# New issue intervals and urgencies for a list schedule, and float32 operands that are no longer used unsplit

## The chip, the cores and the metric

The kernel runs on one core of a Trainium2 chip. The metric is the time of the launch on the device in microseconds (us); the median of several executions is given. Four compute engines matter: TensorE (PE in the profile, with its weight loads apart as PEld) multiplies matrices, VectorE (DVE) and ScalarE (ACT) work element by element, and SyncE (SP) starts most transfers between the chip's memory and the core's buffers. GpSimd (POOL) starts some of the output transfers.

## The reference

The program is a packed attention, whose result is the input of a feed-forward network. Cut to what matters:

```python
q, k, v: (8, 8, 576, 64)      # batches, heads, positions, head size
p:       (8, 8, 32, 64)       # 32 packed queries for each head

def sm_attn(qq, kk, vv):
    s = scale * qq @ kk.T
    a = exp(s - max(s)); a = a / (sum(a) + 1e-09)
    return a @ vv

p_packed = sm_attn(p, k, v)                    # 32 rows for each head
x = sm_attn(q, p_packed, p_packed)             # 576 rows for each head
x = x.transpose(0, 2, 1, 3).reshape(4608, 512) # one row for each token
h = x @ w_in                                   # 512 -> 2048
g = where(h > 0, h, exp(min(h, 0)) - 1)        # ELU
out = g @ w_out                                # 2048 -> 512
```

## The kernel before

**Stages.** For each of 8 batches the kernel does the first attention (scores of the packed queries, maximum, exponentials, transposes on TensorE, products with v), and the second attention's scores and softmax over 32 columns, whose parts are folded with 32x32 transposes on VectorE (`s2` L695, `fold` L703, `smax` L710 to `smul` L732, `unfold` L745). The second attention's last product is not done on its own: the packed rows are multiplied with `w_in` first (`mstep`, L757, giving `m`), so that an h product of the network takes `m` and the softmax weights `a`. Then come h products, ELU and out products. Chunks of the 2048 hidden columns are 128 wide and called f, so there are 16; a batch's 576 tokens are split in two windows of 256 and 320, called halves.

**Products.** TensorE multiplies float32 in a fast rounded form, fp32r. To keep the precision, an operand x is split into a high part `hi` (x rounded) and a low part `lo` (x − hi), and a product becomes three matmuls, hi·hi, hi·lo and lo·hi: `a_hi`, `a_lo` and `m_hi`, `m_lo` in an h product (L1285), `wo` and `g` parts in an out product (L1409, L1410, L1412). An unsplit product takes plain float32 operands instead (L1278 for h, L1395 for out); in the trace each of its matmuls leaves two records. The `hi` part is a cast (L284, mostly on ScalarE), the `lo` part a subtraction on VectorE (`g` L1324, `m` L809, `a` L751).

**ELU.** For each f of a window ScalarE computes relu(−h) (L1292) and its exponential (L1298), and VectorE combines them (L1301); this last step is "the ELU" below. There are two tiles for h, so that the h product two places on writes where the ELU reads.

**Weights.** `w_in` and `w_out` arrive as 64-bit floating-point words, and are converted on the chip in blocks of 128 rows (i0 to i15, o0 to o15): a load on SP (L307), an exponent on VectorE (L312), a sign and a power on ScalarE (L324, L319), then mantissa steps on VectorE (L327, L333), a product of exponent and sign (L340) and the word (L350); for `w_out`, also the parts `hi` (L284) and `lo` (L363).

**Batches 0 and 1, and the rest.** While the weights arrive, batches 0 and 1 are worked on in turns, by the list `VISITS` of (batch, half, f from, f to). Batches 2 to 7 follow whole. From batch 2's second half on, two chunks at a time go through Strassen's scheme (L1048 for h, L1187 for out, operands of g at L1121 and L1130): 21 matmuls of 256 columns instead of 12 of 512 for an out product of the pair. Pairs named in `S_PLAIN` and `S_PLAINS` are plain, with the 12. The operands made from `w_out` for Strassen (L916 to L949) are stored to the chip's memory and loaded again for each use.

**What sets the order.** Every instruction, or short run of them, is recorded by `op(prio, on, fn, deps, take, use, after, mode)`: `on` says on which engines it may run and at what cost, `deps` what it waits for, `take` the tile that it fills. `schedule()` then walks a model of time: of the instructions that may begin, it takes the one of lowest `prio` (the urgency, counted in products of the network), puts it on its engine, and sets when the engine is next idle (`idle_at`, the cost and `GAP`) and when the result may be used (`end`, the cost and `LAG`). The order that results is the static order of each engine's queue; at run time semaphores make instructions wait. Urgencies come from numbers at the top (`T_ATT`, `LI`, `LO`, `TM`, `LOOK` and the like), and `FIRST` sets the order of the first loads.

`F_PLAIN` is the number of `w_out` chunks whose products of batches 0 and 1 are unsplit; `H_PLAIN` names the batches whose first four chunks have unsplit h products. `STAY` and `SWITCH` concern TensorE's changes between two kinds of matmuls.

Of the kernel before, what the change touches and what calls it, by code (L numbers as in the profile page):

```python
# [20 lines left out]
def packed_attention_elu_ffn(  # L21
# [55 lines left out]
    ]  # L77

    T_ATT, T_ATT1 = [11.5, 13.5, 14.0, 15.0, 16.0, 16.0], [-12, -11, -11, -10, -10, -9]
    LI, LO, LM, LOOK = 4.5, 3.0, 2.5, 3.5
    TM = [24.5, 22.0, 25.0, 26.0]

    FIRST = "i0 i1 i2 i3 k v o0 o1 q".split()
    T_S2, STAY, SWITCH = 0, 4, 0.12

    F_PLAIN, H_PLAIN = 4, [0, 1]  # L90
    T_WS, T_AS = 20, 6

    S_PLAIN = [0, 7]
    S_PLAINS = {x: [0] for x in [(3, 1), (4, 0), (4, 1), (5, 0), (5, 1), (6, 0), (6, 1), (7, 0)]}
    T_SW7 = 16
    T_ATTS = [[5, 9, 13.5, 6.5, 13.0, 23.5], [-4, -2, -2, 3, 14.5, 22.0]]
    TMS = [[22, 19.5, 27.0, 27.0], [19, 29, 30.0, 30.5]]

    T_TH, LOOK_T = 1, 1
    S_FIRST, T_SW, T_SL, T_SE, LOOK_S = (2, 1), 17, 10, 5, 6.0

# [43 lines left out]
    class Buf:  # L147
        def __init__(self, ring, make, n=1):
            self.ring, self.make, self.n, self.users, self.t = ring, make, n, [], None

        def released(self, now):
            return all(u.end is not None and u.end <= now for u in self.users)
# [4 lines left out]
    ops = []  # L157
    GAP = {"PE": 0.0, "DVE": -0.03, "ACT": 0.02, "DMA": 0.0, "POOL": 0.0, "CTL": 0.0}
    LAG = {"PE": 0.15, "DVE": 0.1, "ACT": 0.12, "DMA": 2.2, "POOL": 5.0, "CTL": 0.0}
# [12 lines left out]
    def schedule():  # L172

        todo = sorted(ops, key=lambda o: (o.prio, o.n))
        idle_at = {e: 0.0 for e in GAP}
        now, out, mode = 0.0, [], None

        def engine_for(o):

            if any(d.end is None for d in o.after) or any(  # L180
                d.end is None or d.end > now for d in o.deps
            ):
# [5 lines left out]
            spare = 2.0 if any(c.end is None for c in conv_ops) else 0.0  # L188
            e = min(o.on, key=lambda e: max(idle_at[e], now) + o.on[e] + spare * (e == "DVE"))
            return e if idle_at[e] <= now else None  # L190

        while todo:
            for n, o in enumerate(todo[:400]):
                e = engine_for(o)
# [17 lines left out]
                todo.remove(o)  # L212
                break
# [648 lines left out]
    for b in range(B):  # L862
        if b == 0:
            ts = [-40 + n for n in range(5)] + [T_S2]
        elif b < NB0:
            ts = [first_use["b", b] + t for t in T_ATT1]
        else:
            ts = [first_use["b", b] - NS + t for t in (T_ATT if b <= S_FIRST[0] else T_ATTS[b % 2])]
# [9 lines left out]
    for b in range(B):  # L878
        for c in range(NFC):
# [3 lines left out]
            else:  # L883
                t = TM if b <= S_FIRST[0] else TMS[b % 2]
# [18 lines left out]

    def s_need(u):

        return next((i for i, (b, win, _) in enumerate(order) if strassen(b, win) and u not in plain_in(b, win)), None)
# [116 lines left out]
    def strassen_pair(i, b, win, f):  # L1023
# [487 lines left out]
```

## Time and profile before

| | |
|---|---|
| median of 3 runs | 712.98 us |
| lowest, highest | 710.84, 713.93 us |
| span of the profiled execution | 710.4 us, 2.6 below the median |
| TensorE busy | 687.2 us, 97% |
| VectorE busy | 587.7 us, 83% |
| ScalarE busy | 448.1 us, 63% |
| moved by DMA | 140.19 MB, 197 GB/s |

The profile is one execution. Busy time is the time in which an engine had an instruction under way, and an engine's matmuls or vector instructions overlap a little, so that the sum of single durations can be more than the busy time. A "start to start" time is read from two rows of the timeline. In a row, "out<-in" gives the tiles, then the sizes; "x4" is the number of instructions; in brackets or behind the last bar stand the idle time ahead of them and what ended it.

### The profile page before, as it was taken

The numbers are of one execution on the slowest core, as the hardware profiler recorded it, in microseconds if no ns is written. First come the engines' busy times: TensorE is split into PE (matmuls) and PEld (weight loads), VectorE is DVE, ScalarE is ACT, GpSimd is POOL, SyncE is SP. The second block draws the span as 40 slices with busy tenths as digits, with TensorE's granted clock in tenths as the row PEclk, the third lists the DMA queues.
The fourth block names the chain that finished last, engine by engine and source line by source line (L and its number), as shares of the span: only waits on it lengthen the run. The fifth ranks groups of instructions, "written<-read, shape, count | busy, mean of one in ns | idle before, by whom it ended". The sixth has DMA issues, their size and how long they took to land.

```text
span 710.4 us, 15186 instructions
## 1 busy us (share of the span) xinstructions
PE 687.2 (97%) x5688; PEld 573.6 (81%) x5688; DVE 587.7 (83%) x1430; ACT 448.1 (63%) x963; POOL 19.4 (3%) x27
## 2 busy tenths in 40 slices
PE   2799999999999999999999999999999999999997
PEld 1444588887777888899889998889888999899986
DVE  6999998888998889776898799866798889977563
ACT  5777788887666666665466555756556655655532
POOL 0000002111021000000000000000000000000000
PEclk9999999999999999999999999999999999999999
DMA  9846555645748845646867897566867887754600
GB/s 354 291 152 216 165 177 117 140 86 124 215 94 208 285 137 179 179 145 195 297 195 260 280 306 230 185 185 203 266 220 243 278 257 226 210 189 138 204 31 30
DMA packets 72553, 140.19 MB, mean 197 GB/s; under 512 B 7200, under 2 KB 16672, under 8 KB 72224
## 3 DMA queue, kind: packets, MB, share of 16 engines
q1 hardware_dynamic: 69456, 133.72, 58.2%
q0 software_dynamic: 3024, 5.51, 5.5%
q8 instruction: 45, 0.74, 0.4%
q14 instruction: 28, 0.23, 0.1%
HBM read 116.92 MB, written 22.28 MB: 196 GB/s over the span
## 4 chain that ended last, share of the span: by engine, by line
PE 93%; DMA 3%; DVE 2%; ACT 1%; issue 0%; SPq 0%; ACTq 0%
PE psum L1187 29%; PE psum L1048 19%; PE psum L1285 8%; PE psum L1409 6%; PE psum L1410 5%; PE psum L1412 5%; PE psum L1007 5%; PE psum L796 4%; PE psum L1395 4%; PE psum L1278 2%; DMA kvq<-in_qT 2%; PE psum L650 2%; PE psum L624 1%; PE psum L695 1%; DMA k<-in_kT 1%; PE psum L554 1%
## 5 line engine op out<-in xcount | busy, mean ns | idle before, releaser
L1187 PE MATMUL psum<-sw,g 128*128 128x256 f32 x816 | 126.0, 282 | 0.0
L1187 PEld LDWEIGHTS psum<-sw,g 128*128 128x128 f32 x816 | 109.9, 188 | 6.5 <-issue 4.7
L1048 PE MATMUL psum<-a_hi,m_hi 128*128 128x320 f32 (+1 forms) x320 | 97.3, 304 | 0.0
L1048 PE MATMUL psum<-a_lo,m_hi 128*128 128x320 f32 (+1 forms) x320 | 95.4, 298 | 0.0
L1048 PE MATMUL psum<-a_hi,m_lo 128*128 128x320 f32 (+1 forms) x320 | 95.3, 298 | 0.0
L1130 DVE TENSOR_TENSOR g<-w,g 128x896 fp32r<-128x896 f32 (+1 forms) x80 | 82.0, 1026 | 13.6 <-ACT g L284 13.1
L284 ACT CAST g<-w 128x896 fp32r<-128x896 f32 (+1 forms) x80 | 71.2, 890 | 23.9 <-DVE w L1121 15.0
L1187 PE MATMUL psum<-wo_a,g 128*128 128x256 f32 (+1 forms) x390 | 72.8, 318 | 0.0
L1121 DVE TENSOR_TENSOR w<-w 128x128 f32<-128x128 f32 (+1 forms) x204 | 68.1, 334 | 5.0
L1060 ACT ACTIVATE e<-psum 128x320 f32<-128x320 f32 x96 | 42.0, 437 | 44.9 <-PE psum L1048 40.1
L1048 PEld LDWEIGHTS psum<-a_hi,m_hi 128*128 128x128 f32 x320 | 60.4, 189 | 11.3 <-ACT e L1063 5.0
L1292 ACT ACTIVATE e<-psum 128x256 f32<-128x256 f32 (+1 forms) x96 | 38.6, 404 | 43.8 <-PE psum L1285 30.2
L1187 PEld LDWEIGHTS psum<-wo_a,g 128*128 128x128 f32 x390 | 58.7, 189 | 8.0 <-issue 2.6
L1048 PEld LDWEIGHTS psum<-a_lo,m_hi 128*128 128x128 f32 x320 | 60.4, 189 | 1.6
L1048 PEld LDWEIGHTS psum<-a_hi,m_lo 128*128 128x128 f32 x320 | 60.4, 189 | 0.0
L1187 PE MATMUL psum<-wo_b,g 128*128 128x256 f32 (+1 forms) x366 | 59.6, 290 | 0.0
L1187 PEld LDWEIGHTS psum<-wo_b,g 128*128 128x128 f32 x366 | 50.9, 188 | 5.3 <-issue 3.1
L1285 PE MATMUL psum<-a_hi,m_hi 128*128 128x256 f32 (+1 forms) x160 | 49.2, 307 | 0.1
L1055 DVE SCALAR_TENSOR_TENSOR w<-e,psum 128x256 f32<-128x256 f32 x96 | 39.6, 413 | 11.5 <-ACT e L1063 11.1
L1063 ACT ACTIVATE e<-e 128x320 f32<-128x320 f32 x96 | 45.3, 472 | 2.5
L1285 PE MATMUL psum<-a_lo,m_hi 128*128 128x256 f32 (+1 forms) x160 | 46.4, 290 | 0.0
L1285 PE MATMUL psum<-a_hi,m_lo 128*128 128x256 f32 (+1 forms) x160 | 46.4, 290 | 0.0
(140 smaller groups left out, 1436.3 us busy)
## 6 DMA issues: line engine op xcount, KB each, us to landing
sw<-sw_dram SPq DMA_DIRECT2D x272, 256.0 KB, 3.6
raw<-in_w_in SPq DMA_DIRECT2D x16, 512.0 KB, 3.9
kvq<-in_v SPq DMA_DIRECT2D x16, 512.0 KB, 5.2
raw<-in_w_out SPq DMA_DIRECT2D x16, 512.0 KB, 3.5
kvq<-in_kT SPq DMA_DIRECT2D x14, 576.0 KB, 5.0
kvq<-in_qT SPq DMA_DIRECT2D x14, 576.0 KB, 5.9
sw_dram<-sw SPq DMA_DIRECT2D x28, 256.0 KB, 4.1
out<-part POOLq DMA_DIRECT2D x21, 256.0 KB, 5.3
```

Source lines behind the costliest of these rows:

```text
L284: (nc.scalar.copy if e == "ACT" else nc.vector.tensor_copy)(out=out, in_=in_)
L1007: nc.tensor.matmul(acc.t, lhsT=gh.t[:, p * P:(p + 1) * P], rhs=wo(f, q), start=f == n == 0, stop=f == NF - 1 and n == 2,)
L1048: nc.tensor.matmul(ps, lhsT=m_b[p].t[:, g, o:o + P], rhs=st.a.t[q][:, g, cols], start=(n == 0), stop=(n == 3 * G - 1),)
L1055: nc.vector.scalar_tensor_tensor(out=out, in0=e_, scalar=-1.0, in1=ps, op0=ALU.add, op1=ALU.max)
L1060: nc.scalar.activation(out=out, in_=ps, func=AF.Relu, scale=-1.0)
L1063: nc.scalar.activation(out=x, in_=x, func=AF.Exp, scale=-1.0)
L1121: nc.vector.tensor_tensor(out=out, in0=x, in1=y, op=o)
L1130: nc.vector.tensor_tensor(out=g_b.all[:, 7 * P:(7 + b1 - b0) * P], in0=blocks(b0, b1), in1=g_b.all[:, :(b1 - b0) * P].bitcast(F32), op=ALU ...
L1187: nc.tensor.matmul(a.t[:, at * H:at * H + rhs.shape[-1]], lhsT=operand(blk, p), rhs=rhs, start=a.first == u and n == k == 0, stop=a.final ...
L1285: nc.tensor.matmul(ps_b.t[:, :n_tok], lhsT=m_b[x].t[:, g, o:o + P], rhs=st.a.t[y][:, g, cols], start=(n == 0), stop=(n == 3 * G - 1),)
L1292: nc.scalar.activation(out=e_b.t[:, :n_tok], in_=ps_b.t[:, :n_tok], func=AF.Relu, scale=-1.0)
L1409: nc.tensor.matmul(a.t, lhsT=g_b.t[0][:, t], rhs=wo(f, 0), start=first, stop=False)
```

## The change

The schedule's model gets other numbers: `GAP` of VectorE −0.03 to −0.08 and of ScalarE 0.02 to −0.10, `LAG` of TensorE 0.15 to 0.2, of VectorE 0.1 to 0.05 and of ScalarE 0.12 to 0.05. An instruction that can only run on the engine that makes its operand becomes ready as soon as that engine is idle, without the lag. All urgencies are other numbers, some of them given batch by batch now, and two pairs of visits change places. `F_PLAIN` goes from 4 to 0, so that no out product is unsplit (`w_words` is gone), and `H_PLAIN` from [0, 1] to [0], which leaves the unsplit h products of batch 0's first four chunks. The list of plain pairs changes from 12 to 14 pairs, and since batch 3's second half has none, pair 0's Strassen operands are needed too; for that there is a branch in the groups of a plain pair. `Buf.free`, `o.wait` and `s_needs` only keep what was computed anew each time.

```diff
     VISITS = [
-        (0, 0, 0, 4), (0, 1, 0, 4), (1, 0, 0, 4), (1, 1, 0, 8), (0, 1, 4, 8),
-        (1, 0, 4, 8), (0, 0, 4, 12), (0, 1, 8, 12), (1, 0, 8, 12), (1, 1, 8, 16),
-        (0, 1, 12, 16), (1, 0, 12, 16), (0, 0, 12, 16),
+        (0, 0, 0, 4), (0, 1, 0, 4), (1, 0, 0, 4), (1, 1, 0, 8),
+        (0, 1, 4, 8), (1, 0, 4, 8), (0, 0, 4, 12), (0, 1, 8, 12),
+        (1, 0, 8, 12), (0, 1, 12, 16), (1, 1, 8, 16), (0, 0, 12, 16),
+        (1, 0, 12, 16),
     ]
...
-    LI, LO, LM, LOOK = 4.5, 3.0, 2.5, 3.5
+    LI = 3.0
+    LO = 0.0
...
-    FIRST = "i0 i1 i2 i3 k v o0 o1 q".split()
-    T_S2, STAY, SWITCH = 0, 4, 0.12
+    FIRST = "i2 o1 o0 i3 o2 v k i0 q".split()
+    T_S2 = 2.5
+    STAY = 3
+    SWITCH = 0.105
-    F_PLAIN, H_PLAIN = 4, [0, 1]
+    F_PLAIN = 0
+    H_PLAIN = [0]
...
-    S_PLAIN = [0, 7]
-    S_PLAINS = {x: [0] for x in [(3, 1), (4, 0), (4, 1), (5, 0), (5, 1), (6, 0), (6, 1), (7, 0)]}
+    S_PLAIN = []
+    S_PLAINS = {
+        (2, 0): [0], (2, 1): [0, 7], (3, 0): [0, 7], (3, 1): [], (4, 0): [0, 4], (4, 1): [0],
+        (5, 0): [0, 7], (5, 1): [0], (6, 0): [0, 4], (6, 1): [0], (7, 0): [0],
+    }
...
-    GAP = {"PE": 0.0, "DVE": -0.03, "ACT": 0.02, "DMA": 0.0, "POOL": 0.0, "CTL": 0.0}
-    LAG = {"PE": 0.15, "DVE": 0.1, "ACT": 0.12, "DMA": 2.2, "POOL": 5.0, "CTL": 0.0}
+    GAP = {"PE": 0.0, "DVE": -0.08, "ACT": -0.1, "DMA": 0.0, "POOL": 0.0, "CTL": 0.0}
+    LAG = {"PE": 0.2, "DVE": 0.05, "ACT": 0.05, "DMA": 2.2, "POOL": 5.0, "CTL": 0.0}
...
                 idle_at[e] = now + cost + GAP[e]
                 o.start, o.end = now, now + cost + LAG[e] + o.lag
+                for x, needs in o.next:
+                    x.wait -= 1
+                    if needs:
+
+                        x.ready = max(x.ready, idle_at[e] if list(x.on) == [e] else o.end)
...
-                ((0, own(f, 0, 2), 0), (2, own(f + 1, 0, 2), 0)),
+                ((0, own(f, 0, 2), 0), (2, own(f + 1, 0, 2), 0))
+                if 0 in plain_in(b, win) else
+                tuple((blk, own(f + blk // 2, n), n) for n in range(2) for blk in (0, 2)),
```

Lines of the kernel after the change stand 17 further down in the weights and the attention (L350, the word, is L367), 23 further down in the ordinary products (L1301, the ELU, is L1324).

How the instructions move is shown at three places. The first is the start of SP's queue, which starts the loads: `raw` is a weight block, `p`, `k`, `kvq` and `q` are inputs of the attention. Before:

```order
L307 DMA raw<-in_w_in 128x1024 x3
L461 DMA p<-in_pT 128x128
L463 DMA k_123<-in_kT 128x2304
L307 DMA raw<-in_w_in 128x1024
L472 DMA kvq<-in_v 128x2x512
L476 DMA kvq<-in_v 64x256
```

After:

```order
L324 DMA raw<-in_w_in 128x1024
L324 DMA raw<-in_w_out 128x1024 x2
L478 DMA p<-in_pT 128x128
L480 DMA k_124<-in_kT 128x2304
L324 DMA raw<-in_w_in 128x1024
L324 DMA raw<-in_w_out 128x1024
L489 DMA kvq<-in_v 128x2x512
L493 DMA kvq<-in_v 64x256
```

Blocks of `w_out` are among the first three loads now, and one more weight block stands ahead of `v`; `k` still stands behind three.

The second place is VectorE at the second softmax of batch 0's first half, where the scores are folded and the rows' maximum, sum and quotient are taken, with weight conversions between. Before:

```order
L703 STREAM_TRANSPOSE tmp<-psum 128x288
L312 TENSOR_SCALAR ex<-raw 128x512
L703 STREAM_TRANSPOSE tmp<-psum 128x288
L327 TENSOR_SCALAR mi<-raw 128x512
L710 TENSOR_REDUCE mx_343<-tmp 128x18
L333 SCALAR_TENSOR_TENSOR mi<-raw,mi 128x512
L713 TENSOR_TENSOR tmp<-tmp,mx_343 128x576
L340 TENSOR_TENSOR ex<-ex,sg 128x512
```

After:

```order
L720 STREAM_TRANSPOSE tmp<-psum 128x288 x2
L727 TENSOR_REDUCE mx_322<-tmp 128x18
L730 TENSOR_TENSOR tmp<-tmp,mx_322 128x576
L329 TENSOR_SCALAR ex<-raw 128x512
L344 TENSOR_SCALAR mi<-raw 128x512
L350 SCALAR_TENSOR_TENSOR mi<-raw,mi 128x512
L740 TENSOR_REDUCE sm_336<-tmp 128x18
L743 TENSOR_SCALAR sm_336<-sm_336 128x18
L746 RECIPROCAL sm_336<-sm_336 128x18
```

The steps of a softmax, and those of a conversion, stood in turns; now each stands directly behind the one whose result it needs.

The third place is VectorE around the ninth ELU. Before:

```order
L809 TENSOR_TENSOR m_lo<-psum,m_hi 128x2x256
L751 TENSOR_TENSOR a_lo<-q_617,a_hi 128x2x288
L1301 SCALAR_TENSOR_TENSOR g<-e,psum 128x320
L363 TENSOR_TENSOR wo_a<-w_words,wo_a 128x512
L1301 SCALAR_TENSOR_TENSOR g<-e,psum 128x320
L363 TENSOR_TENSOR wo_a<-mi,wo_a 128x512
```

After:

```order
L1347 TENSOR_TENSOR g<-e,g 128x256
L1347 TENSOR_TENSOR g<-half_sb,g 128x64 x2
L357 TENSOR_TENSOR ex<-ex,sg 128x512
L1324 SCALAR_TENSOR_TENSOR e<-e,psum 128x320
L367 SCALAR_TENSOR_TENSOR w_in_sb<-mi,ex 128x4x128
L1324 SCALAR_TENSOR_TENSOR e<-e,psum 128x320
L1347 TENSOR_TENSOR g<-e,g 128x320
L1347 TENSOR_TENSOR g<-half_sb,g 128x64
```

An ELU of these chunks wrote the whole operand `g`; now it writes `e`, a cast makes `g`'s high part, and one or two subtractions (L1347, before L1324) make the low one.

More of the change, by code (lines that the diff above doesn't have):

```diff
@@ L73, in packed_attention_elu_ffn @@
     VISITS = [
[3 rows of a table removed]
-    ]
-    T_ATT, T_ATT1 = [11.5, 13.5, 14.0, 15.0, 16.0, 16.0], [-12, -11, -11, -10, -10, -9]
-    LI, LO, LM, LOOK = 4.5, 3.0, 2.5, 3.5
-    TM = [24.5, 22.0, 25.0, 26.0]
-    FIRST = "i0 i1 i2 i3 k v o0 o1 q".split()
-    T_S2, STAY, SWITCH = 0, 4, 0.12
-    F_PLAIN, H_PLAIN = 4, [0, 1]
-    T_WS, T_AS = 20, 6
-    S_PLAIN = [0, 7]
-    S_PLAINS = {x: [0] for x in [(3, 1), (4, 0), (4, 1), (5, 0), (5, 1), (6, 0), (6, 1), (7, 0)]}
[L97 to L102, printed above, removed]
[4 rows of a table added]
+    ]
+    T_ATT = [11.5, 13.5, 13.0, 16.5, 14.0, 20.0]
+    T_ATT1 = [-8.5, -9.5, -6.0, -7, -13.5, -11.5]
+    LI = 3.0
+    LO = 0.0
+    LM = 3.5
+    LOOK = 5.0
+    TM = [25.0, 23.5, 27.0, 25.0]
+    FIRST = "i2 o1 o0 i3 o2 v k i0 q".split()
[4 more added lines that the diff above has]
+    H_PLAIN = [0]
+    T_WS = 26
+    T_AS = 13
+    S_PLAIN = []
[3 more added lines that the diff above has]
+    }
+    T_SW7 = 17
+    T_ATTS = {3: [-4, -2, -2, 3, 14.5, 22.0], 4: [5.5, 9, 13.5, 7.0, 13.0, 28.5], 5: [-3.5, -2, -2.5, 3, 14.5, 22.0], 6: [5, 9, 13.5, 6.0, 13.0, 25.5], 7: [-4, -2, 2, -1, 14.5, 26.0]}
+    TMS = {3: [19, 29, 29.5, 30.5], 4: [22, 19.5, 27.0, 27.0], 5: [23, 29, 30.0, 31.0], 6: [24, 19.5, 25.0, 27.0], 7: [21.5, 29, 26.5, 28.5]}
+    T_TH = 1
+    LOOK_T = 1.5
+    S_FIRST = (2, 1)
+    T_SW = 8.5
+    T_SL = 10.5
+    T_SE = 15.0
+    LOOK_S = 5.0
     class Ring:
@@ L149, in __init__ @@
             self.ring, self.make, self.n, self.users, self.t = ring, make, n, [], None
+            self.free = False
         def released(self, now):
-            return all(u.end is not None and u.end <= now for u in self.users)
+            self.free = self.free or all(u.end is not None and u.end <= now for u in self.users)
+            return self.free
     class Op:
@@ L172, in schedule @@
     def schedule():
+        for o in ops:
+            o.wait, o.ready, o.next = len(o.deps) + len(o.after), 0.0, []
+        for o in ops:
+            for d in o.deps:
+                d.next.append((o, True))
+            for d in o.after:
+                d.next.append((o, False))
         todo = sorted(ops, key=lambda o: (o.prio, o.n))
         idle_at = {e: 0.0 for e in GAP}
-        now, out, mode = 0.0, [], None
+        now, out, mode, converted = 0.0, [], None, 0
+        conv = set(conv_ops)
         def engine_for(o):
-            if any(d.end is None for d in o.after) or any(
-                d.end is None or d.end > now for d in o.deps
-            ):
+            if o.wait or o.ready > now:
                 return None
@@ L186, in engine_for @@
                     return None
-            spare = 2.0 if any(c.end is None for c in conv_ops) else 0.0
+            spare = 2.0 * (converted < len(conv_ops))
             e = min(o.on, key=lambda e: max(idle_at[e], now) + o.on[e] + spare * (e == "DVE"))
@@ L193, in schedule @@
             for n, o in enumerate(todo[:400]):
+                if o.wait or o.ready > now:
+                    continue
                 e = engine_for(o)
@@ L212, in schedule @@
                 todo.remove(o)
+                converted += o in conv
                 break
@@ L867, in packed_attention_elu_ffn @@
         else:
-            ts = [first_use["b", b] - NS + t for t in (T_ATT if b <= S_FIRST[0] else T_ATTS[b % 2])]
+            ts = [first_use["b", b] - NS + t for t in (T_ATTS[b] if b in T_ATTS else T_ATT)]
         sts[b] = attention(b, ts)
@@ L883, in packed_attention_elu_ffn @@
             else:
-                t = TM if b <= S_FIRST[0] else TMS[b % 2]
+                t = TMS[b] if b in TMS else TM
                 mstep(b, c, 0, 1, first_use["b", b] - NS + t[c])
@@ L902, in strassen @@
         return S_FIRST <= (b, win) < (B - 1, 1)
+    s_needs = [
+        next((i for i, (b, win, _) in enumerate(order) if strassen(b, win) and u not in plain_in(b, win)), None)
+        for u in range(NF // 2)
+    ]
     def s_need(u):
-        return next((i for i, (b, win, _) in enumerate(order) if strassen(b, win) and u not in plain_in(b, win)), None)
+        return s_needs[u]
     def strassen_weights(u):
```

## The prediction

> **What bounds the kernel now.** I read the totals on the page first, then the windows, the chain of waits, the groups by line and shape, and the timeline where start-to-start times are wanted.
>
> ```profile
> span 710.4 us, 15186 instructions
> PE 687.2 (97%) x5688; PEld 573.6 (81%) x5688; DVE 587.7 (83%) x1430; ACT 448.1 (63%) x963; POOL 19.4 (3%) x27
> core 0: us, PE busy (x) PEld busy (x) DVE busy (x) ACT busy (x) POOL busy (x), PEclk, DMA share, GB/s
> 0.00:35.00 35.00, 16.98 (x301) 10.96 (x301) 28.60 (x67) 22.65 (x46) 0.69 (x6) 0.95 0.88 325
> 35.00:103.30 68.30, 67.86 (x383) 39.53 (x379) 64.79 (x147) 53.30 (x117) 0.00 (x0) 1.00 0.55 178
> 103.30:218.20 114.90, 114.13 (x903) 90.36 (x903) 99.55 (x234) 84.92 (x208) 16.17 (x18) 1.00 0.57 129
> 0.00:218.20 218.20, 198.97 (x1567) 140.85 (x1568) 192.94 (x447) 160.87 (x370) 16.86 (x24) 0.99 0.61 175
> 250.00:706.00 456.00, 455.87 (x3855) 405.65 (x3854) 367.15 (x910) 265.70 (x533) 0.00 (x0) 1.00 0.64 204
> ```
>
> The first row is the span, 2.6 us below the median of 712.98; all differences below are added to that median. The window rows give busy time by engine. From 250 to 706 us TensorE is never idle (455.87 of 456), at the full granted clock (1.00), with VectorE at 81%: there only less TensorE work can shorten the run. Ahead of 218 us two engines are nearly full. TensorE is full from 35 us on (67.86 of 68.30, 114.13 of 114.90), and VectorE leaves 25.3 us of 218.2 unused, of which only 3.5 lie between 35 and 103 us. 218.2 us is where the 65th ELU of batches 0 and 1 starts on VectorE. The h product two later writes into the tile that this ELU reads, so TensorE can't be past it.
>
> **TensorE's products.** In the chain of waits (start, us, engine, line) whole products stand as single steps:
>
> ```profile
> 47.71 1.08 PE psum L1278 x4
> 68.12 0.86 PE psum L1278 x4
> 82.51 1.72 PE psum L1395 x4
> 84.23 0.71 PE psum L1285 x6
> 91.04 0.24 PE psum L1409
> 91.27 0.23 PE psum L1410
> 91.50 0.47 PE psum L1412 x2
> ...
> 103.79 0.41 PE L1285 MATMUL psum<-a_hi,m_hi 128*128 128x320 f32 x1
> 104.04 0.31 PE L1285 MATMUL psum<-a_lo,m_hi 128*128 128x320 f32 x1
> 104.19 0.31 PE L1285 MATMUL psum<-a_hi,m_lo 128*128 128x320 f32 x1
> ```
>
> An unsplit out product is half of the four records of 82.51: 0.86 us. Split it is one matmul each of L1409, L1410 and L1412: 0.24 + 0.23 + 0.47/2 = 0.705. All 36 are split now: 36 × 0.155 = −5.6. An unsplit h product is four records: 0.86 for 256 columns, 1.08 for 320. Split it is six matmuls: 0.71, and 6 × 0.147 = 0.88 (104.04 to 104.19 is 0.15 for one). Batch 1's first four chunks are split now in both windows, four products of each width: 4 × 0.15 + 4 × 0.20 = −1.4.
>
> The order counts 157 switches between modes on TensorE, 165 before. The first matmul behind a switch takes 0.25 to the next start (103.79 to 104.04) instead of 0.15, so −0.8 in all.
>
> ```profile
> 302.18 2.79 PE psum L1187 x12
> 360.85 2.51 PE psum L1187 x21
> ```
>
> Among the later batches a plain pair (12 matmuls) costs 2.79 and a Strassen pair 2.51. There are 14 plain pairs instead of 12: +0.6. Pair 0's Strassen weights are made now as well, which is four more stores of 256 KB, with eight fewer loads; DMA is 64% busy in 250 to 706, nothing there waits for it in the windows, so 0.
>
> So TensorE has 5.6 + 1.4 + 0.8 − 0.6 = 7.2 us less to do. Were it the only bound, that would be the gain: 705.8.
>
> **What VectorE pays ahead of the 65th ELU.** Every split operand needs its low part, a subtraction on VectorE (the high part is a cast, mostly on ScalarE, 74% busy ahead of 218 us, which covers it). Rows of groups: count | busy us, mean ns | idle before.
>
> ```profile
> L1324 DVE TENSOR_TENSOR g<-e,g 128x256 fp32r<-128x256 f32 x68 | 28.6, 421 | 4.6 <-ACT g L284 4.0
> L1324 DVE TENSOR_TENSOR g<-e,g 128x320 fp32r<-128x320 f32 x12 | 5.8, 486 | 1.2 <-ACT g L284 1.2
> L1324 DVE TENSOR_TENSOR g<-half_sb,g 128x64 fp32r<-128x64 f32 x12 | 2.6, 219 | 0.9 <-ACT g L284 0.7
> L809 DVE TENSOR_TENSOR m_lo<-psum,m_hi 128x512 fp32r<-128x512 f32 x12 | 8.2, 689 | 3.3 <-ACT m_hi L284 3.3
> L949 DVE TENSOR_TENSOR sw<-w,sw 128x256 fp32r<-128x256 f32 x28 | 11.1, 417 | 0.2
> L916 DVE TENSOR_TENSOR w<-wo_b 128x1024 f32<-128x1024 f32 x4 | 4.9, 1218 | 0.0
> ```
>
> By the order, ahead of the 65th ELU stand now: 12 × 0.421 + 4 × 0.486 + 4 × 0.219 = 7.9 for the new g parts (L1324), 2 × 0.689 = 1.4 for m (L809); and, moved here from behind, 9 × 0.417 + 2 × 1.218 = 6.2 of Strassen weights (L949, L916) and about 3.3 of smaller ones, two of 0.685 and the rest of 0.42; other steps −1.1. That is +17.7 us busy in 40 instructions more. Rows overlap, though:
>
> ```profile
> 4.45 0.43 DVE L312 TENSOR_SCALAR ex<-raw 128x512 uint16<-128x512 uint16 x1 [3.58 <-DMA raw<-in_w_in]
> 4.79 0.42 DVE L327 TENSOR_SCALAR mi<-raw 128x512 uint32<-128x512 uint32 x1
> 5.25 0.69 DVE L333 SCALAR_TENSOR_TENSOR mi<-raw,mi 128x512 f32<-128x512 uint32 x1
> 5.86 0.42 DVE L340 TENSOR_TENSOR ex<-ex,sg 128x512 bf16<-128x512 bf16 x1
> ...
> 12.28 0.76 DVE L523 TENSOR_REDUCE mx<-psum 128x1 f32<-128x576 f32 x1 [0.86 <-PE psum L513]
> ...
> 20.90 0.43 DVE L340 TENSOR_TENSOR ex<-ex,sg 128x512 bf16<-128x512 bf16 x1 [0.55 <-ACT sg L324]
> ...
> 34.88 0.42 DVE L1301 SCALAR_TENSOR_TENSOR g<-e,psum 128x256 f32<-128x256 f32 x1 [0.25 <-ACT e L1298]
> ...
> 217.57 0.76 DVE L563 TENSOR_REDUCE mx<-psum 128x2 f32<-128x576 f32 x1 [0.77 <-ACT tmp L284]
> 218.25 0.41 DVE L1301 SCALAR_TENSOR_TENSOR e<-e,psum 128x256 f32<-128x256 f32 x1
> ```
>
> L327 starts 0.34 us after L312, before that one's 0.43 are over; L333 reads L327's result and starts 0.46 after a 0.42 instruction. So an instruction that needs nothing of the one directly ahead starts 0.08 before its end, one that does starts 0.04 after it: 0.12 dearer. Start to start the 40 instructions cost 17.7 − 40 × 0.083 = +14.4. And the new order puts many dependents directly behind their producer: 100 ahead of the 65th ELU, 25 before; 75 × 0.12 = +9.0.
>
> Here a rule of the Trainium skill speaks against this term. "VectorE: DVE Perf Modes", section "The DRAIN you can't avoid", states that eight copies with a semaphore after each take 13.88 us and with one only after the last also 13.88, so "the semaphore costs nothing extra here". By it the 9.0 would be nothing and the 65th ELU could come some 9 us earlier, near rival B. Here 0.46 stands against 0.34 for instructions of one length, so the trace doesn't agree with it, and the trace decides.
>
> Now the waits. Ahead of 218.25 VectorE has 54 waits, the first the 3.58 and the last the 0.77 in the rows above. The four before 35 us (3.58, 0.86, 0.55, 0.25, together 5.2) come from the first loads and the first scores; as the first scores' keys stand behind three weight loads on SP in both orders, I keep them. If the other 50 close, each lets the next instruction start 0.083 earlier, 4.1 in all. The floor for the 65th ELU is then 192.9 + 14.4 + 9.0 + 5.2 − 4.1 = 217.4 us. At the other end VectorE waits as it does from 35 to 103 us, 3.5 of 68.3 or 5.1%: 9.4 us over the 183 us behind 35 us, and the ELU comes at 226.8. I take a quarter of that, 219.7: the 5.1% is with TensorE full beside it, which has 3% in hand now, but the two still follow one another through two h tiles, so not all of it goes.
>
> ```profile
> 173.05 0.71 PE L624 MATMUL psum<-ident,tmp 128*128 128x128 f32 x5
> ...
> 226.74 1.39 PE psum L650 x80
> ```
>
> Against 218.25 the 65th ELU is 1.5 us late. TensorE's saving ahead of there (7.0 of products, and some 0.3 of the switches) turns into waits for ELUs. Behind it TensorE is full as before, with +0.6 for plain pairs, four out products that the order brings behind it (4 × 0.705 = +2.8), ten transposes and 40 products of an attention that it brings ahead of it (two steps of five, 0.71 each, and half of the 80 in 1.39: −2.1), and −0.5 of switches: +0.8. Sum: 712.98 + 1.5 + 0.8 = 715.3.
>
> At the very start, SP brings v behind one weight load more, so the second softmax's first fold may come 1.6 us later (512 KB at the 325 GB/s of the first window). I cost it at nothing: VectorE has conversions to do meanwhile. If it doesn't, the bound is the +1.6, inside the waits' range. The successor rule and the new GAP and LAG only act through the orders counted here.
>
> **Rivals.** A measurement of this kernel tells a difference from none at about 0.5%, 3.6 us: 709.4 and 716.5 are the limits.
>
> A, the forecast: VectorE sets the pace up to the 65th ELU and hands TensorE's saving back. Waits of 0 to 2.0% of 183 us put the ELU at 217.4 to 221.0, and the time at 712.9 to 716.5.
>
> B, faster: the dependents don't cost here what the few rows of before show, or VectorE's work moved ahead isn't needed on the path since the ELUs come before it in time. Without the 9.0 the 65th ELU could come at 211 or earlier, TensorE stays full and the whole 7.2 shows: 705.8. The rule of the Trainium skill above leads to this one. For it speaks that every TensorE cost falls, that TensorE is 97% busy, and that from 250 us on it is the sole bound. Against it: 217.4 is a floor with every wait closed. Between, 705.8 to 709.4.
>
> D, slower: VectorE's waits stay, at over 2.0% of 183 us (3.6 us), which is the point from which it decides. Place: from 35 us to the 65th ELU. Each per cent costs 1.8 us; 5.1% gives 712.98 + (226.8 − 218.25) + 0.8 = 722.3, 3.5% gives 719.4. For it: the planner now lets a VectorE result be used at the very end of its producer's slot, 0.12 too early at each of 100 pairs, so it places the other engines' work for a VectorE up to 12 us faster than the rows allow; and where orders are fixed, TensorE and VectorE then wait by turns. Against it: a TensorE with 7 us in hand, and ScalarE at 74%.
>
> **How the numbers follow.** A 0.41, B 0.25, D 0.34. A's own range is 711.0 to 716.5 (some two microseconds below its floor for the error of the tallies). The whole range takes in B's full gain and D up to 4.3% of waits: 705.5 to 721.0; what is left out is the end of D and a B that gains more, under 2 in 10. Faster 0.25, same 0.41, slower 0.34, from the same cases. That B gets a quarter in spite of the floor is for the 12 us of closing waits and tallies that no row can vouch for in another order.
>
> **What would show it.** Right: no unsplit out product (L1395's counterpart) in the groups, split out products at 0.7 us; VectorE over 93% busy from 35 us to the 65th ELU, that ELU at 217 to 221 us, and TensorE with 5 to 9 us idle between 35 and 218 us that it didn't have, ended by ELUs or by g parts on VectorE; from 250 us on TensorE full again. The step on dependents is right if the rows of the ex and w product (L357 to L367) stand 0.04 apart from end to start. Wrong: the 65th ELU at 211 or earlier (B), or at 222 and later with VectorE under 90% busy (D); or TensorE idle anywhere behind 250 us, which I cost at nothing.

## The result, and the profile after

The changed kernel takes 730.04 us (729.56 to 730.48, 4 runs), the kernel before 713.45 beside it. The ratio is 1.0243, with a 95% interval of 1.0214 to 1.0271: slower by 17 us, where no measurable change was forecast. The profiled execution spans 727.5 us, 17.1 more than before. Below are the page's head and then the windows, with the stretches and columns that were shown of before.

```profile
span 727.5 us, 15282 instructions
PE 690.5 (95%) x5722; PEld 580.7 (80%) x5722; DVE 605.0 (83%) x1443; ACT 458.9 (63%) x994; POOL 19.5 (3%) x27
...
0.00:35.00 35.00, 15.30 (x226) 7.88 (x227) 29.49 (x63) 20.65 (x40) 0.69 (x6) 0.87 0.87 323
35.00:103.30 68.30, 65.22 (x495) 49.71 (x494) 65.80 (x156) 55.68 (x132) 0.00 (x0) 0.99 0.44 149
103.30:218.20 114.90, 112.43 (x966) 87.82 (x965) 112.50 (x260) 95.07 (x233) 15.20 (x18) 1.00 0.66 171
0.00:218.20 218.20, 192.95 (x1683) 145.41 (x1684) 207.79 (x477) 171.40 (x403) 15.90 (x24) 0.98 0.62 189
250.00:706.00 456.00, 448.31 (x3775) 393.74 (x3772) 368.40 (x887) 266.06 (x537) 0.00 (x0) 1.00 0.62 200
```

Two places show it. Ahead of 218 us VectorE is fuller (207.79 against 192.94) and TensorE emptier (192.95 against 198.97), as forecast. From 250 to 706 us, where TensorE was never idle, it now is for 7.7 us, and VectorE is no busier there (368.40 against 367.15). Those 7.7 us are a lower bound of what is lost: matmul records overlap (one of 0.31 us is followed by the next start after 0.15), so a short wait leaves no idle time. A better ruler is the start of the first Strassen product. Two timelines give it, first before and then after; the second begins with the 65th ELU (rows: start us, us, engine, line).

```profile
252.26 0.31 PE L1048 MATMUL psum<-a_hi,m_hi 128*128 128x320 f32 x1
```

```profile
221.47 0.41 DVE L1324 SCALAR_TENSOR_TENSOR e<-e,psum 128x256 f32<-128x256 f32 x1
...
254.14 0.31 PE L1069 MATMUL psum<-a_hi,m_hi 128*128 128x320 f32 x1
```

So the early stage is 1.9 us longer. That is not clear of chance: before and the six variants of it below whose order is the same up to 250 us (`b_pad`, `b_pad60`, `b_pad64`, `b_pad128`, `b_together`, `b_together60`) have this start anywhere from 251.3 to 254.6 us. The stretch from the first Strassen product to the end, "the Strassen stage" below, grew from 710.4 − 252.3 = 458.1 us to 727.5 − 254.1 = 473.4. These 15.3 us are nine tenths of the loss. Both are read from one execution of each kernel, and so are all stages below; before and the two variants with memsets, `b_pad` and `b_pad60`, lie 1.4 us apart in it (458.1, 459.5, 458.4), so single differences of 1 to 3 us say little.

TensorE's waits from 250 to 706 us, as the profile puts them down, were none before. After there are eleven lines with 7.2 us in all, 6.2 of them for VectorE and 1.0 for ScalarE; the first three (us in total, times, longest):

```profile
PE psum L1069 <- DVE half_sb L1076: 1.8, 4, 1.1
PE psum L1069 <- DVE e L1076: 1.7, 2, 1.4
PE psum L813 <- DVE m_lo L826: 1.0, 2, 0.7
...
```

L1076 is the Strassen stage's ELU (L1055 before). It has two parts for a tile of h, and the tile is free for the next h product when the second has read it. The longest of these waits, in the chain of waits:

```profile
484.62 0.96 ACT tmp L598 x3
485.59 0.02 issue
485.61 0.18 DVE ri L562
485.79 0.02 issue
485.81 0.17 DVE ri L565
485.98 0.42 DVE w L1076
486.40 0.02 issue
486.43 0.30 DVE w L1142
486.73 0.02 issue
486.75 0.43 DVE w L1142
487.19 0.02 issue
487.21 0.29 DVE w L1142
487.50 0.14 DVE e L1076
487.64 0.14 issue
487.78 1.12 PE psum L1069 x6
```

On VectorE the ELU stands behind a softmax step (`ri`) that itself waits for ScalarE, and between the ELU's two parts stand three sums (L1142) that need the first part's result. TensorE waits for the second part. This is one wait; how far it stands for the rest is asked below.

### The profile page after: what moved, and what is told of

Read it like the earlier page. It is cut to its first block, busy times and chain, and to the rows that moved or that the text cites. A ratio compares the mean times of both kernels' runs of the same rounds, so it can differ in the third digit from the quotient of the medians.

```text
span 727.5 us, 15282 instructions
## 1 busy us (share of the span) xinstructions
PE 690.5 (95%) x5722; PEld 580.7 (80%) x5722; DVE 605.0 (83%) x1443; ACT 458.9 (63%) x994; POOL 19.5 (3%) x27
## 4 chain that ended last, share of the span: by engine, by line
PE 50%; DVE 35%; ACT 7%; DMA 4%; issue 3%; SPq 0%; ACTq 0%; DVEq 0%
PE psum L1210 17%; PE psum L1069 12%; PE psum L1028 4%; DVE w L1142 4%; PE psum L1308 4%; PE psum L1432 3%; DVE m_lo L826 3%; PE psum L1433 3%; PE psum L1435 3%; DVE w L1076 3%; DVE g L1347 2%; DVE g L1151 2%; DVE e L1324 2%; ACT g L301 2%; PE psum L813 1%
## 5 line engine op out<-in xcount | busy, mean ns | idle before, releaser
L1210 PE MATMUL psum<-sw,g 128*128 128x256 f32 x792 | 123.7, 283 | 0.4 <-DVE m_lo L826 0.3
L1210 PEld LDWEIGHTS psum<-sw,g 128*128 128x128 f32 x792 | 107.1, 189 | 9.9 <-issue 6.1
L1142 DVE TENSOR_TENSOR w<-w 128x128 f32<-128x128 f32 (+1 forms) x198 | 66.5, 336 | 6.4
L1210 PE MATMUL psum<-wo_a,g 128*128 128x256 f32 (+1 forms) x387 | 71.1, 315 | 0.0
L1210 PE MATMUL psum<-wo_b,g 128*128 128x256 f32 (+1 forms) x375 | 64.6, 302 | 0.0
L1210 PEld LDWEIGHTS psum<-wo_b,g 128*128 128x128 f32 x375 | 53.8, 188 | 7.9 <-issue 4.7
L1324 DVE SCALAR_TENSOR_TENSOR e<-e,psum 128x256 f32<-128x256 f32 (+1 forms) x96 | 41.0, 428 | 22.6 <-ACT e L1321 22.3
L1308 PE MATMUL psum<-a_hi,m_hi 128*128 128x256 f32 (+1 forms) x176 | 52.6, 299 | 1.9 <-DVE e L1324 1.0
L1308 PE MATMUL psum<-a_lo,m_hi 128*128 128x256 f32 (+1 forms) x176 | 51.3, 291 | 0.4 <-DVE a_lo L768 0.4
L1076 DVE SCALAR_TENSOR_TENSOR w<-e,psum 128x256 f32<-128x256 f32 x96 | 39.9, 416 | 13.7 <-ACT e L1084 12.9
L1308 PE MATMUL psum<-a_hi,m_lo 128*128 128x256 f32 (+1 forms) x176 | 51.1, 291 | 0.0
```

The lines of the kernel that those rows point to most:

```text
L1076: nc.vector.scalar_tensor_tensor(out=out, in0=e_, scalar=-1.0, in1=ps, op0=ALU.add, op1=ALU.max)
L1142: nc.vector.tensor_tensor(out=out, in0=x, in1=y, op=o)
L1210: nc.tensor.matmul(a.t[:, at * H:at * H + rhs.shape[-1]], lhsT=operand(blk, p), rhs=rhs, start=a.first == u and n == k == 0, stop=a.final ...
L1308: nc.tensor.matmul(ps_b.t[:, :n_tok], lhsT=m_b[x].t[:, g, o:o + P], rhs=st.a.t[y][:, g, cols], start=(n == 0), stop=(n == 3 * G - 1),)
L1324: nc.vector.scalar_tensor_tensor(out=out, in0=e_b.t[:, cs], scalar=-1.0, in1=ps_b.t[:, cs], op0=ALU.add, op1=ALU.max)
```

## The experiments

One measure is used beside the times, worked out from a trace and the program's semaphores: for each matmul from 250 to 700 us that waits for VectorE, its lead, the time from the end of the VectorE instruction to the matmul's start. Before, a tenth of 255 leads are under 0.66 us and 4 are under 0.15; after, 36 of 246 are under 0.15, more than a tenth. "Pairs" are VectorE instructions directly behind the one whose result they need.

The theories: (1) the pairs' 0.12 us each; (2) the new urgencies, which leave too little lead; (3) the split products; later (4) the planner's new model (GAP, LAG and successor rule), on the idea that its old, higher prices had been a margin; and, of the pairs, (5) that their time on VectorE counts or (6) the order.

**The split products alone**, `b_split`:

```diff
-    F_PLAIN, H_PLAIN = 4, [0, 1]
+    F_PLAIN, H_PLAIN = 0, [0]
```

> The kernel before, with its own urgencies, prices and rule, in which only the products change: no out product is unsplit, and the unsplit h products of batch 1 are split (F_PLAIN 0, H_PLAIN [0]). Dependent pairs 304, as before 303. By my prediction's sum without the term of the dependents and without the Strassen operands brought ahead: the 65th ELU 0 to 7 us earlier, 706 to 713 us. Theory 3 (the low parts alone make VectorE the bound and cost the time after the change): 716 to 725 us, with the 65th ELU at 221 us or later.

Measured: 713.13 us, ratio 1.0010 (0.9998 to 1.0022). The 65th ELU comes at 219.3 us, the first Strassen product at 254.2, and the Strassen stage is 458.1, as before. So theory 3 falls, and so does the hope for 706: TensorE's saving is given back by the split alone, without the Strassen operands brought ahead and without new pairs (28 in the first 218 us, before 29). Its window:

```profile
35.00:218.00 183.00, 176.37 (x1379) 136.93 (x1377) 171.78 (x409) 144.03 (x345) 15.93 (x18) 1.00 0.56 153
```

Neither engine is full there (TensorE 96%, VectorE 94%). TensorE is busy for 5.4 us less than before and VectorE for 7.6 more (181.79 and 164.14 before); that the two then wait by turns is my reading, and no run shows it apart.

**The successor rule undone in after**, `x_rule`:

```diff
-                        x.ready = max(x.ready, idle_at[e] if list(x.on) == [e] else o.end)
+                        x.ready = max(x.ready, o.end)
```

> The kernel after, with one line of its planner undone: an instruction on the same engine as its operand's producer is ready at the producer's end plus the lag again, 0.13 us later in the model than the next independent one. All urgencies, GAP, LAG and split products are those of after. The order has 321 dependent pairs on VectorE (after 497, before 303). Theory 1: most of the loss behind 250 us goes, 714 to 721 us. Theory 2: the urgencies still set the lead, 725 to 732 us. Orders differ everywhere, so chance alone may move it by a few us either way.

Measured: 720.13 us, 1.0099 (1.0073 to 1.0124). First Strassen product 254.8, stage 464.6: 8.8 of the 15.3 us are gone, with the urgencies of after. It counts against theory 2 alone. In the first 218 us 28 pairs are left of 100, and VectorE's waits up to the 65th ELU grow from 6.1 to 11.3; the 65th ELU comes at 219.2, 2.3 us earlier, where 72 × 0.12 = 8.6 would have come off by the pairs.

**The whole old model in after**, `x_model`, with the edit above and

```diff
-    GAP = {"PE": 0.0, "DVE": -0.08, "ACT": -0.1, "DMA": 0.0, "POOL": 0.0, "CTL": 0.0}
-    LAG = {"PE": 0.2, "DVE": 0.05, "ACT": 0.05, "DMA": 2.2, "POOL": 5.0, "CTL": 0.0}
+    GAP = {"PE": 0.0, "DVE": -0.03, "ACT": 0.02, "DMA": 0.0, "POOL": 0.0, "CTL": 0.0}
+    LAG = {"PE": 0.15, "DVE": 0.1, "ACT": 0.12, "DMA": 2.2, "POOL": 5.0, "CTL": 0.0}
```

> The kernel after with the planner's model of before: GAP and LAG as before, and a same-engine successor ready at the producer's end plus the lag. Urgencies, products and plain pairs are those of after. Theory 4 (new: the old prices were too high by some 0.05 us for each VectorE instruction and by more for ScalarE, so the planner ordered for slower engines and real results came with time in hand; the new prices leave none): TensorE is idle for under 2 us between 250 and 706 us and the time is 710 to 717 us, below the 720.1 of the kernel in which the successor rule alone was undone. Theory 2 (the new urgencies take the lead away): 722 to 732 us with 5 us or more idle.

Measured: 727.35 us, 1.0206 (1.0179 to 1.0233): above the expectation, but all of it early. The first Strassen product comes at 262.8, and the stage behind it is 462.0.

**The whole new model in before**, `b_model`: GAP and LAG the other way round, and `schedule()` of after with

```diff
+                        x.ready = max(x.ready, idle_at[e] if list(x.on) == [e] else o.end)
```

> The kernel before with the planner's model of after: new GAP, LAG and successor rule; urgencies, unsplit products and plain pairs are those of before. 588 dependent pairs on VectorE instead of 303. Theory 4, and theory 1 with it: TensorE idle for 5 to 12 us between 250 and 706 us and 722 to 732 us. Theory 2: TensorE full there, 711 to 716 us.

Measured: 750.47 us, 1.0526 (1.0504 to 1.0547), far above: first Strassen product at 269.1, stage 477.0. From 250 to 700 us TensorE is busy for 437.83 us, before for 449.87.

**New GAP and LAG alone in before**, `b_gap`, without the successor rule:

```diff
+    GAP = {"PE": 0.0, "DVE": -0.08, "ACT": -0.1, "DMA": 0.0, "POOL": 0.0, "CTL": 0.0}
+    LAG = {"PE": 0.2, "DVE": 0.05, "ACT": 0.05, "DMA": 2.2, "POOL": 5.0, "CTL": 0.0}
```

> The kernel before with the new GAP and LAG alone; a same-engine successor waits for the lag as before, so a dependent costs 0.13 us more than an independent one in the model too, about what the trace shows. 357 dependent pairs instead of 303. Theory 1 (it is the pairs): at most 54 x 0.12 = 6 us, 712 to 718 us. Theory 4 (it is the margin of the prices): 718 to 727 us, with TensorE idle between 250 and 706 us for 4 us or more.

Measured: 727.51 us, 1.0220 (1.0191 to 1.0249); first Strassen product 257.8, stage 467.1, 9.0 over before, with 221 pairs in 250 to 700 us against 195. 26 × 0.12 = 3 us of pairs can't make 9, so theory 1 is not enough for this run.

**The later urgencies and plain pairs of before in after**, `x_late2`:

```diff
+    S_PLAIN = [0, 7]
+    T_SW7 = 16
+    LOOK_T = 1
+    T_SW = 17
+    T_SL = 10
+    T_SE = 5
+    LOOK_S = 6.0
...
```

The lines left out are `S_PLAINS`, `T_ATTS` and `TMS` of before.

> The kernel after with the urgencies of before for everything behind batch 2 (the attention and m of batches 3 to 7, the Strassen operands, the lead of 6 instead of 5 products) and the plain pairs of before; model, early urgencies and split products are those of after. 537 dependent pairs, 450 of them behind the 65th ELU. Theory 2: TensorE is full again behind 250 us, 713 to 719 us. Theories 1 and 4: TensorE idle for 5 us or more there, 723 to 733 us.

Measured: 734.41 us, 1.0311 (1.0286 to 1.0337); first Strassen product 252.9, stage 478.9. Theory 2 falls for this stage: with the old urgencies it is longer still.

Put together, the Strassen stage in us:

| model of the planner | urgencies of before | urgencies of after |
|---|---|---|
| old GAP, LAG and rule | 458.1 | 462.0 |
| new GAP and LAG, old rule | 467.1 | 464.6 |
| new GAP, LAG and rule | 477.0 | 473.4 |
| old GAP, new LAG and rule (`a_gapold`, below) | — | 465.8 |

The columns also differ in the split products, which with the old model change nothing in this stage (`b_split`), and in the plain pairs. On top of the new GAP the successor rule adds 9 to 10 us in each column; the new GAP and LAG alone add 9.0 or 2.6. With the urgencies of after, taking back either the rule or GAP removes 7.6 or 8.8 of the 11.4 us, so they can't be priced one by one: most of the loss comes from the two together. The urgencies, with the plain pairs, lengthen the stage by 3.9 under the old model and shorten it under the new one. VectorE's and ScalarE's numbers were always changed together, so no run says whose matter.

**The old model for the later batches only**, `x_staged`: after, whose planner uses GAP, LAG and rule of before for urgencies from 64 on.

```diff
+                late = o.prio >= 2 * NS
-                idle_at[e] = now + cost + GAP[e]
+                idle_at[e] = now + cost + (GAP0 if late else GAP)[e]
...
-                        x.ready = max(x.ready, idle_at[e] if list(x.on) == [e] else o.end)
+                        x.ready = max(x.ready, idle_at[e] if list(x.on) == [e] and not late else o.end)
```

> The kernel after whose planner keeps the new GAP, LAG and successor rule for work of batches 0 and 1, and takes those of before for all work of urgency 64 and later (batch 2 on). Urgencies, products and plain pairs are those of after; 85 dependent pairs ahead of the 65th ELU as after (87), 274 behind it (after 410, before 276). If the model of the later stage alone makes the loss there: the first Strassen product at 253 to 256 us as after, the stretch from there 460 to 465 us, 714 to 721 us in all. If the loss comes from the early stage or from the urgencies: 471 us or more, 725 to 732 us.

Measured: 719.67 us, 1.0089 (1.0062 to 1.0116). First Strassen product and TensorE's window:

```profile
255.84 0.31 PE L1072 MATMUL psum<-a_hi,m_hi 128*128 128x320 f32 x1
...
250.00:700.00 450.00, 448.68 (x3807) 397.51 (x3806) 363.99 (x903) 265.82 (x534) 0.00 (x0) 1.00 0.63 203
```

The stage is 717.8 − 255.8 = 462.0, and a tenth of its leads are under 0.60 us. So 11.4 of the 15.3 us go with the planner's model for the later stage, with the early model, the urgencies and the products left as they are. The other 3.9 belong to what stays different, the urgencies and the plain pairs (0.6 by the prediction's sum).

**Pairs taken apart in after**, `a_apart`: a pass behind the planner moves a VectorE instruction by a few places where that parts a pair and the model has it ready; nothing else moves.

```diff
-        for o, e in schedule():
+        for o, e in apart(schedule()):
```

> The kernel after, with the same schedule on every engine, but on VectorE an instruction is moved by a few places wherever that separates a dependent pair (an instruction directly behind the one whose result it needs) and the model has it ready: 390 such pairs instead of 497, 26 fewer ahead of the 65th ELU and 81 fewer behind. Theory 1 (each pair costs 0.12 us, and so VectorE comes late for TensorE also behind 250 us): up to 107 x 0.12 = 13 us less, and since not all of it lies on the path, 718 to 725 us. Theory 2 (the new urgencies give VectorE's results too little lead, whatever stands behind what): 728 to 731 us, no change. TensorE's idle time between 250 and 706 us, 7.7 us after the change, falls below 4 by theory 1 and stays by theory 2.

Measured: 732.95 us, 1.0276 (1.0253 to 1.0299). In 250 to 700 us 246 pairs are left of 309, and the stage is 475.8, 2.4 longer. Theory 1 fails here: fewer pairs, and no gain; that what was moved between now stands ahead of urgent results is a guess. Sums stand between the two parts of 6 of 95 ELUs, in after of 39; so the pattern of the chain above is not the whole cause either. By the traces it is 10 before, 19 in `x_model` and `x_staged`, and 40 in `b_model`, `x_late2` and `b_together`, so it mostly goes with the loss; but `b_gap` has 7 and a stage of 467.1, and `a_gapold` 39 and 465.8.

**Pairs brought together in before**, `b_together` and, with the first 60, `b_together60`:

```diff
+            seq[v[0]:n] = seq[v[0] + 1:n] + [seq[v[0]]]
```

> The kernel before, with the same schedule, but from batch 2's second half on VectorE's instructions that stood between an instruction and the next one's operand are moved behind the pair, one place each: 395 dependent pairs there instead of 276 (the kernel after has 410). Nothing else moves; no urgency, no price and no product is changed. Theory 1: up to 119 x 0.12 = 14 us more, 720 to 727 us, and TensorE idle between 250 and 706 us. Theory 2: 712 to 715 us, TensorE full as before.

> The kernel before with the first 60 instead of 115 pairs brought together on VectorE (344 pairs behind the 65th ELU, 395 with 115, 276 before). The loss with 115 was 10 us of the stretch from the first Strassen product to the end. Theory 5: about half of it, 462 to 465 us. Theory 6: it hangs on which few instructions are moved, anything from 458 to 468.

Measured: 720.86 us, 1.0116 (1.0096 to 1.0136), stage 468.1; and 719.72, 1.0111 (1.0068 to 1.0155), stage 465.3. No price or urgency is touched; with 115 a tenth of the leads are under 0.16 us, with 60 under 0.36. By themselves the two runs fit theory 1; the next ones part time from order. The first 60 pairs cost 7.2 us of the stage, the other 55 only 2.8 (by the medians of the whole time, 1.1).

**VectorE's time alone in before**: at the same 115 places a small instruction is put in and nothing is moved. `b_pad` and `b_pad60` used a memset of one column:

```diff
+            if id(o) in pads:
+                nc.vector.memset(warm, 0.0)
```

> The kernel before with its order untouched; at the 115 places on VectorE where an instruction was moved behind a pair to bring the pair together, a memset of one column of a tile that nobody reads is put in instead. That takes VectorE's time without moving anything; by the smallest rows of VectorE (0.15 to 0.17 us long, some 0.1 to 0.19 start to start) 115 of them are 10 to 20 us. Theory 5 (TensorE waits because VectorE has too little time in this stage, so 0.12 us for each of 115 pairs is enough): the stretch from the first Strassen product to the end grows from 458 to 465 to 475 us, as with the pairs brought together (468). Theory 6 (what was lost there is the order: an urgent result now stands behind others): 457 to 461 us, and 711 to 716 in all.

> The same with the first 60 of these memsets. Theory 5: about half of what 115 cost, 461 to 467 us for the stretch. Theory 6: 457 to 460 us.

Measured: 713.14 us, 0.9997 (0.9980 to 1.0013), and 714.02, 1.0013 (0.9993 to 1.0033). The stages are 459.5 and 458.4. They don't tell: VectorE's busy time in 250 to 700 us is 365.72 with 115 memsets against 365.11, so they took next to nothing. A sum over 64 or 128 columns of a constant tile takes more:

```diff
+                nc.vector.tensor_reduce(out=warm, in_=ident[:, :64], op=ALU.add, axis=AX.X)
```

> The kernel before with its order untouched and, at the same 115 places on VectorE, a maximum-like reduction (a sum over 64 columns of a constant tile into one column that nobody reads) instead of the memset, which had taken no time of its own. By the row of a reduction over 576 columns (0.68 us start to start) I estimate 0.08 to 0.15 us start to start each, 9 to 17 us in all, about what 115 pairs cost at 0.12. Theory 5 (VectorE's time is what is short): the stretch from the first Strassen product to the end grows from 458 to 464 to 470 us. Theory 6 (it is the order): 457 to 461 us.

> The same with 128 columns: by my estimate 0.15 to 0.22 us each, 17 to 25 us in all, more than the pairs of the kernel after cost there. Theory 5: 468 to 478 us for the stretch. Theory 6: 458 to 464 us, since VectorE still waits for other engines for more than that in this stage (79 us in the kernel before).

Measured: 715.78 us, 1.0051 (1.0033 to 1.0070), and 719.96, 1.0098 (1.0073 to 1.0122). The timeline of the first shows one:

```profile
301.44 0.21 DVE L1056 SCALAR_TENSOR_TENSOR e<-e,psum 128x64 f32<-128x64 f32 x1
301.57 0.21 DVE L1501 TENSOR_REDUCE warm<-ident 128x1 f32<-128x64 f32 x1
301.70 1.06 DVE L1122 TENSOR_TENSOR w<-w 128x128 f32<-128x128 f32 x3
```

It costs 0.13 start to start, as a pair does; 115 are 14.8 us of VectorE, and the stage is 461.0, 2.9 longer. With 128 columns, 0.195 each and 22.4 us in all, it is 463.3, 5.2 longer. So a fifth to a quarter of VectorE's extra time reaches the stage (by the ratios of the whole time, 3.6 and 7.0 us, a quarter to a third). The 90 more pairs of `b_together` in 250 to 700 us are 10.8 us of VectorE's time and lengthened the stage by 10.0: by that share I estimate 2 to 3 of it as time, and the rest as order. Both runs lie in theory 6's ranges, the first at the very edge.

**Other sizes of the margin.** The first two edits are in after (`a_lag`, `a_gapold`), the others in before (`b_margin`, and `b_lag_split`, which has the split products too):

```diff
+    LAG = {"PE": 0.2, "DVE": 0.35, "ACT": 0.35, "DMA": 2.2, "POOL": 5.0, "CTL": 0.0}
...
+    GAP = {"PE": 0.0, "DVE": -0.03, "ACT": 0.02, "DMA": 0.0, "POOL": 0.0, "CTL": 0.0}
...
+    GAP = {"PE": 0.0, "DVE": 0.02, "ACT": 0.07, "DMA": 0.0, "POOL": 0.0, "CTL": 0.0}
...
+    GAP = {"PE": 0.0, "DVE": -0.08, "ACT": -0.1, "DMA": 0.0, "POOL": 0.0, "CTL": 0.0}
+    LAG = {"PE": 0.2, "DVE": 0.55, "ACT": 0.55, "DMA": 2.2, "POOL": 5.0, "CTL": 0.0}
```

> The kernel after with the planner's LAG of VectorE and ScalarE raised from 0.05 to 0.35 us; GAP, the successor rule, urgencies and products stay, and so do the dependent pairs on VectorE (486, after 497). The planner then holds every consumer on another engine 0.3 us later, as a lead in hand. Theory 4 as a matter of lead: waits of TensorE for VectorE that end with under 0.15 us to spare fall from 36 to under 20, the stretch from the first Strassen product to the end shrinks from 473 to 462 to 468 us, and the time is 716 to 724 us. Theory 1 (the pairs): the stretch stays at 471 to 476 us and the time at 727 to 733 us.

> The kernel after with GAP of before (VectorE -0.03, ScalarE 0.02) and everything else of after, the successor rule and the short LAG too: 485 dependent pairs. Theory 4 as a matter of prices (each VectorE instruction charged 0.05 us too much is what kept results early): the stretch from the first Strassen product to the end shrinks from 473 to 463 to 468 us, time 716 to 725 us. Theory 1: 471 to 476 us and 727 to 733 us.

> The kernel before with still higher prices: GAP of VectorE 0.02 instead of -0.03 and of ScalarE 0.07 instead of 0.02; nothing else. Theory 4: behind the first Strassen product TensorE is full already, so nothing can come there, 457 to 460 us; ahead of it the schedule is planned for slower engines than the chip has, which may cost: 711 to 720 us. Theory 1 says the same as to the later stretch (280 pairs there against 276).

> The kernel before with GAP as traced (the new one), without the successor rule, with LAG of VectorE and ScalarE at 0.55 us, and with no unsplit out product and the unsplit h products of batch 0 alone; urgencies and plain pairs of before. 308 dependent pairs. If a lead in LAG does what the high prices did, the stretch from the first Strassen product to the end is 457 to 462 us, where the new GAP and LAG alone had 467, and the time 706 to 718 us; if only the high prices do it, 465 to 470 us and 718 to 728 us.

Measured: 735.09, 740.05, 726.53 and 749.69 us; ratios 1.0305 (1.0290 to 1.0321), 1.0379 (1.0356 to 1.0401), 1.0184 (1.0167 to 1.0202) and 1.0515 (1.0497 to 1.0532). Their stages are 471.9, 465.8, 462.5 and 476.5, so the two in after do shorten it, by 1.5 and 7.6, though all four lose 7 to 20 us ahead of it (first Strassen product at 261.0, 274.1, 262.3 and 271.3). All four miss the time expected by theory 4. Of the stages only that of `a_gapold` lies in theory 4's range; that of `a_lag` lies in theory 1's. The last one misses both of its ranges: an explicit lead in LAG was no substitute. And still higher prices cost 4.4 in the stage, so "the higher, the better" isn't the rule.

In some kernels TensorE's granted clock is lower too, which the stages above don't take apart. From 35 to 218 us it averages 0.93 in `a_gapold`, 0.96 in `b_lag_split` and 0.97 in `x_model`, and 1.00 before and after; in `b_lag_split` it is also 0.97 from 280 to 400 us, which by my estimate is 0.03 × 120 = 3.6 us of its stage. In `x_model` the drop (0.77 from 120 to 140 us) comes behind a stretch in which TensorE is busy for 14.33 of 20 us. No run tells whether the drops make the losses or follow from them.

Over all kernels the stage goes with the shortest leads. Where a tenth of them are under 0.58 to 0.68 us it is 458 to 462 us (before, `b_split`, both memset kernels, `x_model`, `x_staged`); with 0.15, 473 to 479 (after, `a_apart`, `b_model`, `x_late2`); with 0.16 to 0.38 it lies at 461 to 472, but for `b_lag_split` with 476.5. That is a correlation: leads are short wherever TensorE waits, whatever made it, so it shows where the time went and not why.

No kernel here beats the one before.

## Why the prediction was wrong

By its steps:

- TensorE's work: right. No record on `w_words` is left, 32 records of unsplit h products remain (the eight products of batch 0), and in the first 218.2 us TensorE is busy for 6.0 us less, with no time gained.
- VectorE ahead of the 65th ELU: 221.5 us against the forecast 219.7. The busy time ahead of it is 210.96 us (0 to 221.5); the waits are 11 with 6.1 us together, where I had 7.5, and the pairs 100, as counted. That is just outside the 217 to 221 that I gave as a sign of being right. The sum had a slip here: of the 25.3 us that VectorE is idle before, 23.5 are in the 54 waits, and the floor starts from busy time and keeps waits alone, so it leaves out the other 1.8. With them it gives 221.5, but with more waiting and less work than came, so that figure is partly luck. The price of a pair was right: where the word (L367) stands directly behind the product of exponent and sign (L357), it starts 0.034 us after that one's end, in all 22 places. Another step of a conversion shows it too, 0.46 start to start:

```profile
100.28 0.42 DVE L344 TENSOR_SCALAR mi<-raw 128x512 uint32<-128x512 uint32 x1
100.74 0.69 DVE L350 SCALAR_TENSOR_TENSOR mi<-raw,mi 128x512 f32<-128x512 uint32 x1
```

VectorE is busy for 181.47 of the 186.5 us from 35 us to there, 97%; I had said over 93%. TensorE's new idle time between 35 and 218 us is 4.3 us (177.45 busy of 183, before 181.79), just under the 5 to 9 forecast. At the first Strassen product the kernel is 1.9 us late, where the sum had 2.3 for the end. That agreement is luck in good part: the sum's parts were 1.5 up to the 65th ELU and 0.8 behind it; measured are 3.2 and, from there to the first Strassen product, −1.3, and kernels of the same early order lie up to 3.3 us apart. Rival B didn't come. The Trainium skill's statement in "VectorE: DVE Perf Modes", "The DRAIN you can't avoid", that the semaphore costs nothing extra, doesn't hold for these pairs (0.46 us against 0.34), but B failed without them too, by `b_split`.

- But the reason for it was only half right. `b_split` gives the saving back with no new pairs and no operands brought ahead, and `x_rule` takes 72 pairs out for 2.3 us. The term of 9.0 for the pairs was right as VectorE's time and wrong as the path's: with the pairs gone, VectorE waits 5.2 us longer.
- **The step that failed** is "Behind it TensorE is full as before". I read 81% for VectorE in 250 to 706 us as room, and let the new GAP, LAG and successor rule "only act through the orders counted here", but counted the orders up to the 65th ELU alone. For the Strassen stage the sum had 0.6 us, for the plain pairs, and nothing for waits; measured are 15.3, with VectorE as idle as before, and 11.4 of them go with the planner's model there (`x_staged`). The prediction's own tests named this ("TensorE idle anywhere behind 250 us"). Rival D came nearest with a planner that places work for a VectorE faster than the real one, but put it between 35 us and the 65th ELU. That this is how the model does its harm is likely and not shown: `b_together` makes such a loss with the old model, by order alone, and more lag in the model didn't undo it.
- The range ended at 721.0, for D with 4.3% of waits; nothing in it stood for the Strassen stage.

What stays open: which instructions in the new order do the most harm, and whether VectorE's or ScalarE's new numbers place them so. The ELU parted by sums is one case; `a_apart` undoes most of it and gains nothing.

## What to carry to other kernels

Prices that are nearer to the trace need not give a better order. Here the new model for the later stage made it 11.4 us longer, and a tenth of TensorE's leads were under 0.15 us, where with the old one they were under 0.60; yet neither more lag nor still higher prices brought the time back. So after a change of a planner's prices, look at the bottleneck's idle time and at the leads in every stage. Urgencies and a model of time belong together as well: to the first Strassen product, each set took 252 and 254 us with its own model, and crossed they took 263 and 269; undoing the successor rule alone left the new ones at 254.8. And an engine that is busy for 81% of a stage isn't spare: count its new order in every stage where it feeds the bottleneck, before costing it at nothing.

## What the runs showed of the hardware

A one-column memset on VectorE (115 in `b_pad`, 59 ns each by the group's row) between larger instructions took no time that the kernel's time shows (ratio 0.9997, 0.9980 to 1.0013):

```profile
L1501 DVE MEMSET warm<- 128x1 f32 x115 | 6.8, 59 | 0.0
```

Reductions of 64 and 128 columns, 210 and 276 ns long, took 0.13 and 0.195 us start to start, the usual 0.08 less than their length.
